# A copy in place of one of three transfers of V's block sums, halved query loads, and another written order in an attention and two-MLP kernel

## The chip, the cores and the metric

The kernel runs on one core of one Trainium2 chip. The metric is device time in microseconds (us) of one execution. Three runs of the kernel before gave 610.78, 613.39 and 611.55 us: the median is 611.55 us.

## The reference

Everything is float32. Attention with a narrow window and block summaries comes first, then two MLPs (scaling factors of the inputs left out):

```python
def _attn_ref(q, k, v):                      # (2, 8, 768, 64)
    k_sum = k.reshape(B, H, nb, 32, D).max(axis=3)      # 24 block maxima of K
    v_sum = v.reshape(B, H, nb, 32, D).mean(axis=3)     # 24 block means of V
    scores_l = scale * q @ k.T, kept where |i - j| < 16, else -1e9
    scores_s = scale * q @ k_sum.T + log(32)
    a = softmax(concat([scores_l, scores_s], -1))
    return a @ concat([v, v_sum], 2)

def _moe_ref(x, w_in, w_out):                # x (1536, 512), w_in (512, 2048)
    h = x @ w_in
    return (h * sigmoid(h)) @ w_out

def _moe2_ref(x, w_a, w_b, w_out):           # w_a, w_b (512, 1536)
    return (x @ w_a * (x @ w_b)) @ w_out
```

The heads of the attention's output are laid side by side to make the x of the first MLP, whose output is the x of the second.

## The kernel before

**Attention steps.** The attention is cut into 24 steps: 2 batches times 12 blocks of 64 queries, all 8 heads in a step. A step n is a string of small pieces, each a word in the table ORDER: `sc:n` (TensorE, "PE": scores, line 415, with the mask of some steps added by a product, line 409), `sm:n` (VectorE, "DVE": mask and row maximum), `ex:n` (ScalarE, "ACT": exponentials, line 459), `rs:n` (DVE: one over the row sum), `no:n` (GpSimd, "POOL", or DVE: scaling, line 474), `tr:n` (PE: transposes into `pt`, line 480), `pc:n` (copy of them into `pts`), `av:n` (PE: product with the values, line 495), `xh:n` and `xl:n` (the result split into a high and a low part). Scores of two steps share banks, and so do the products `av` of two steps.

**What must be there first.** K and Q arrive as 256 sequence rows at a time (`LKq`, `LQq`, `LQ`), are put in place by copies (`br`), transposed on PE (`tk`, `tq`, line 276, four transposes a word) and copied out in windows (`wk`) or scaled (`bq`, tile `qb`, or `qbm` for the second set). The block means of V come from four loads `LG:b:g` (line 329, two heads each, tiles `vg`), which `sv` sums partly on DVE or POOL (line 338: three halving additions, or one when four terms are left to PE), and which `mv` reduces on PE (line 352, tile `vsum`). `kv` then copies the 24 rows of means into the tile `vw0`.

**The value tiles.** Step n multiplies with `vw[n % 4]`: rows 0 to 95 are the window of V, loaded anew for each step (`LV`, line 369); rows 96 to 119 are the 24 block means of the batch. `kv` fills these in `vw0` alone; `PV:b:i` spreads them to `vw1`, `vw2`, `vw3` by a transfer inside the chip's memory on SyncE's queue ("SP", line 361). The tiles and their last rows live for the whole batch.

**The first MLP** is woven into the attention: `m1:i` (line 591, 12 matmuls of 512 columns; the first two units in halves of 256, `m1:1:0` and `m1:1:1`), `sg`, `gh`, `gl` (its activation, split in high and low), and `m2:i` (line 624, 12 matmuls). Their weights come as words that must be decoded: `LI`/`LO` load, `da` (ACT, line 535), `du` and `dj` (DVE) make a float, `hi` and `lo` split it; `SP` writes a decoded output weight back for the later blocks of tokens. `m1:i` needs the x parts of all eight steps of its block, a half only those of four.

**The order** of all this is the table ORDER near the top of the file, word by word; every engine and SP's queue takes its own instructions in that order, and nothing is moved later. `dm:i:y` puts four transposes of a constant into an unread bank on PE (`keep_warm`, line 926); `dm:i:n` does nothing. After the table's last word (`att`) comes the rest: the first MLP's last units, and the second MLP, in loops that the change does not touch.

Of the kernel before, what the change touches and what calls it, by code (L numbers as in the profile page):

```python
# [32 lines left out]
ex:1 sm:2 rs:1 ex:2 dm:2:n sc:0:n sc:3:s sm:3 mv:0:0:512:4 LG:0:2 LG:0:3 sv:0:3:4:v LQ:0:1 tq:0:1:0 ex:3 bq:0:1:0:v sm:0 ex:0
mv:0:1:0:1 mv:0:3:0:4 sv:0:2:1:p mv:0:2:0:1 kv:0:0:v tq:0:1:1 no:1:p bq:0:1:1:a tr:1 pc:1:a rs:3 pk:0:1:p sc:4:n LV:1 rs:2
rs:0 LI:1 no:3:p tr:3 sc:7:n sc:5:s sm:4 pc:3:v LV:3 dm:7:y LI:2 sm:7 du:in:1 da:in:1 no:2:p tr:2 PV:0:1 ex:4 PV:0:3 no:0:p
rs:4 no:4:p sm:5 av:3:n av:1:s tr:0 ex:7 LQ:0:2 rs:7 ex:5 pc:2:a xh:1:v xh:3:v xl:3 sc:6:n tq:0:2:0 LV:0 xl:1 tq:0:2:1 sm:6
pc:0:a dm:8:n du:in:2 dj:in:1 no:7:p tr:7 da:in:2 ex:6 LV:2 av:0:n bq:0:2:1:a tr:4 dj:in:2 PV:0:2 av:2:n pk:0:2:p bq:0:2:0:v
sc:11:n sc:9:s rs:5 dm:6:n no:5:p xh:0:a xl:0 rs:6 pc:7:a xh:2:a xl:2 sc:8:n LI:0 dm:11:n pc:4:a sc:10:s tr:5 sm:11 sm:9
no:6:p tr:6 hi:in:1:p sm:10 LV:7 av:7:n dm:9:n LV:4 av:4:s LV:5 lo:in:1:p ex:11 LV:6 pc:5:a av:5:n rs:11 no:11:p sm:8 xh:7:v
xl:7 pc:6:a da:in:0 xh:5:a av:6:n dm:4:n xh:6:a xh:4:a tr:11 LK:1:1 ex:8 su:10:v ex:10 m1:1:0 xl:4 ex:9 LI:4 xl:6 xl:5 m1:1:1  # L40
hi:in:2:v LQ:1:0 rs:10 du:in:0 dj:in:0 hi:in:0:v lo:in:0:v lo:in:2:p m1:2 ok:1 du:in:4 tk:1:1:1 sg:1:p gh:1:v gl:1:v tq:1:0:0
sg:2:p tk:1:1:0 tq:1:0:1 da:in:4 dj:in:4 hi:in:4:v LI:3 du:in:3 lo:in:4:v LI:7 LK:1:0 da:in:3 dj:in:3 bq:1:0:1:a rs:8
mk:1:1:0 du:in:7 m1:0:0 m1:0:1 no:8:p da:in:7 LK:1:2 LO:1 bq:1:0:0:a sg:0:v mk:1:1:1 pc:11:a wk:1:1:0:a no:10:p wk:1:1:1:a
dj:in:7 hi:in:7:v lo:in:7:p gh:2:p gh:0:v m1:4 gl:0:v tk:1:0:0 mk:1:0:0 tr:8 hi:in:3:a tk:1:2:0 rs:9 wk:1:2:0:a wk:1:0:0:a
pc:8:a tk:1:0:1 mk:1:0:1 gl:2:p no:9:v da:out:1 LI:13 sg:4:p da:in:13 LV:8 LI:6 lo:in:3:p LV:9 tk:1:2:1 mk:1:2:1 wk:1:2:1:a
# [1151 lines left out]
```

## Time and profile before

| what | value |
|---|---|
| median of three runs | 611.55 us |
| the profiled execution's own time | 610.3 us |
| its span, first to last instruction | 608.5 us |
| PE busy | 598.3 us (98%) |
| DVE busy | 390.2 us (64%) |
| ACT busy | 283.3 us (47%) |
| POOL busy | 270.9 us (45%) |
| bytes moved by DMA | 97.82 MB, mean 161 GB/s |
| granted clock of PE | 1.0 |

A busy share is a mean over stages that differ. PE's small share of idle time is what is left to win or to lose; where in the span it lies is read from the rows below.

### The profile page before, as it was taken

Reading aid. Unit: us, or ns where it says so; the run is one execution under the profiler, and the core shown is the slowest. Engines: PE = TensorE matmul, PEld = TensorE weight load, DVE = VectorE, ACT = ScalarE, POOL = GpSimd, SP = SyncE. Lnnn points to the kernel's source line nnn. Section 1 sums busy time; section 2 is a strip of 40 time slices with the busy share of each in tenths; the row PEclk is TensorE's granted clock in tenths of the full one; section 3 lists DMA queues with packets and bytes.
Section 4 is the critical chain, followed back from the end, with each engine's and each line's share of the span. In section 5 each row is a group of like instructions: output and inputs, shape, how many; then the busy total and the mean of one; then the engine's idle time right before and its main releaser. Section 6 shows DMA issues by size and latency. Waiting matters only on the chain.

```text
span 608.5 us, 10110 instructions
## 1 busy us (share of the span) xinstructions
PE 598.3 (98%) x3652; PEld 525.3 (86%) x3652; DVE 390.2 (64%) x775; ACT 283.3 (47%) x625; POOL 270.9 (45%) x265
## 2 busy tenths in 40 slices
PE   6999999999999999999999999999999999999997
PEld 6788888888788888888888999999999999988886
DVE  6889999878344444577576856694858567454212
ACT  5988778464445144545555313252423223234221
POOL 6745312123342222354457666392956657334220
PEclk9999999999999999999999999999999999999999
DMA  9999987883122427665664105362543512277303
GB/s 238 209 256 254 294 259 210 248 270 103 50 62 59 138 70 225 214 201 191 206 193 155 43 23 179 126 219 101 174 159 112 182 36 87 90 236 296 122 0 139
DMA packets 90538, 97.82 MB, mean 161 GB/s; under 512 B 39016, under 2 KB 68456, under 8 KB 90488
## 3 DMA queue, kind: packets, MB, share of 16 engines
q1 hardware_dynamic: 90344, 97.04, 52.7%
...
q10 hardware_dynamic: 144, 0.13, 0.1%
HBM read 73.79 MB, written 23.07 MB: 159 GB/s over the span
## 4 chain that ended last, share of the span: by engine, by line
PE 95%; DMA 2%; DVE 1%; SPq 1%; ACT 1%; issue 0%; DVEq 0%
PE h L591 22%; PE y L624 22%; PE bankh L835 14%; PE bankg L835 14%; PE ol L882 11%; PE o L858 5%; PE av L495 2%; PE pt L480 1%; PE sc L415 1%; DMA vg<-in_v_dram 1%; DMA st_in<-in_moe_w_in_dram 1%; DVE sm L445 1%; PE qt L276 1%; SPq L253 1%; ACT sm L459 0%; PE kt L276 0%
## 5 line engine op out<-in xcount | busy, mean ns | idle before, releaser
L591 PE MATMUL h<-x,w_in 128*128 128x512 f32 (+1 forms) x600 | 139.4, 383 | 0.0
L624 PE MATMUL y<-g,w_out 128*128 128x512 f32 x576 | 138.5, 391 | 0.0
L591 PEld LDWEIGHTS h<-x,w_in 128*128 128x128 f32 x600 | 108.3, 188 | 21.7 <-issue 0.3
L624 PEld LDWEIGHTS y<-g,w_out 128*128 128x128 f32 x576 | 107.4, 188 | 22.3 <-issue 0.2
L568 POOL TENSOR_TENSOR w_out<-re_out,w_out 128x512 fp32r<-128x512 f32 x38 | 53.9, 1419 | 109.9 <-ACT w_out L151 91.2
L882 PE MATMUL ol<-w_out,plh 128*128 128x512 f32 x188 | 57.8, 389 | 0.0
L606 DVE TENSOR_TENSOR g<-h,g 128x512 fp32r<-128x512 f32 x31 | 21.4, 690 | 42.3 <-ACT g L151 42.0
L568 POOL TENSOR_TENSOR w_out<-w_out,w_out 128x512 fp32r<-128x512 f32 x18 | 25.9, 1451 | 41.1 <-ACT w_out L151 29.9
L599 ACT ACTIVATE h<-h 128x512 f32<-128x512 f32 x31 | 18.1, 583 | 55.2 <-PE h L591 55.2
L800 POOL TENSOR_TENSOR ab<-sum,ab 128x384 f32<-128x384 f32 x24 | 27.3, 1146 | 33.4 <-DVE sum L797 33.4
L882 PEld LDWEIGHTS ol<-w_out,plh 128*128 128x128 f32 x188 | 35.3, 188 | 7.3
L151 ACT CAST w_out<-re_out 128x512 fp32r<-128x512 f32 x35 | 21.8, 621 | 32.9 <-issue 27.0
L871 DVE TENSOR_TENSOR pll<-pl,plh 128x1024 fp32r<-128x1024 f32 x12 | 17.4, 1449 | 30.5 <-ACT plh L870 30.5
L882 PE MATMUL ol<-w_out,pll 128*128 128x512 f32 x94 | 36.6, 389 | 0.0
L858 PE MATMUL o<-w_out,p 128*128 128x512 f32 x108 | 28.5, 393 | 0.0
L835 PE MATMUL bankh<-yhT,wab 128*128 128x384 f32 x96 | 28.2, 334 | 0.0
L545 DVE SCALAR_TENSOR_TENSOR w_out<-w_out,u_out 128x512 uint32<-128x512 uint32 x28 | 23.8, 855 | 5.3 <-ACT w_out L535 3.8
L778 ACT COPY sum<-bankh 128x384 f32<-128x384 f32 x12 | 5.8, 480 | 39.3 <-PE bankh L835 39.3
L474 POOL TENSOR_TENSOR sm<-sm,st 128x480 f32<-128x480 f32 x15 | 15.2, 1027 | 18.2 <-DVE st L470 12.5
L568 POOL TENSOR_TENSOR w_in<-w_in,w_in 128x512 fp32r<-128x512 f32 x10 | 13.4, 1341 | 22.1 <-DVE w_in L153 10.5
L818 ACT CAST p<-ab 128x384 fp32r<-128x384 f32 x12 | 6.2, 514 | 35.0 <-POOL ab L800 17.8
L858 PEld LDWEIGHTS o<-w_out,p 128*128 128x128 f32 x108 | 19.9, 187 | 2.8
...
## 6 DMA issues: line engine op xcount, KB each, us to landing
...
```

The lines of the kernel that those rows point to most:

```text
L151: nc.scalar.copy(o, i)
L545: nc.vector.scalar_tensor_tensor(bits, bits, 3, u_t.pop((kind, f)), op0=ALU.logical_shift_left, op1=ALU.bitwise_or)
L568: engine.tensor_tensor(w[:, 1], w32_t[kind, f], w[:, 0].bitcast(F32), op=ALU.subtract)
L591: nc.tensor.matmul(h_ps[i][:, cols], win_t[f][:, a, c * P:(c + 1) * P], x_t[n][:, steps, m, c, :], start=(idx == 0), stop=(idx == 3 * NK - 1))
L599: nc.scalar.activation(sg_t[i], ps, AF.Silu)
L606: engines[engine].tensor_tensor(g_t[i][:, 1], sg_t.pop(i), g_t[i][:, 0].bitcast(F32), op=ALU.subtract)
L624: nc.tensor.matmul(y_ps[n, c], wout_t[i][:, a, c * P:(c + 1) * P], g_t[i][:, m, :], start=(f == 0 and (a, m) == (0, 0)), stop=(f == N1 - 1 ...
L800: engines["v" if k == 6 else "p"].tensor_tensor(at, x, at, op=ALU.mult)
L835: nc.tensor.matmul((A, B)[b], weights(u, a, s, s + 1)[:, 0, c * P:(c + 1) * P], yc_t[q, y][m][:, c, :], start=(idx == 0 and not more), sto ...
L858: nc.tensor.matmul(o_ps[t], g[:, a, c:c + P], w[:, m], start=(begins and (a, m) == (0, 0)), stop=(ends and (a, m) == PARTS[-1]))
L871: nc.vector.tensor_tensor(l, x, h.bitcast(F32), op=ALU.subtract)
L882: nc.tensor.matmul(late_o[j], late_p[f][a][:, j * P:(j + 1) * P], wo2_t[N2 + f][:, m], start=(f == 0 and (a, m) == (0, 0)), stop=(f == N2 ...
```

## The change

It does four things. `put_vsum` may copy by an engine, and the word `pv:0:1:a` makes the copy into `vw1` of the first batch one of ACT; the transfers to `vw2` and `vw3`, and all three of the second batch, stay. The first queries are loaded as two transfers of four heads each (`LQq:0:0:0 LQq:0:0:1`), as the first keys were already. The table ORDER is written anew from end to end: other places, and at many words another engine (the last letter). And seven `dm` words have a `y` instead of four, which makes 12 more transposes.

```diff
 ORDER = """
-LKq:0:0:0 LKq:0:0:1 qz br:k:0:0:0:v c1 dm:0:y br:k:0:0:1:a tk:0:0:0 tk:0:0:1 dm:5:n c3 ok:0 LKq:0:2 LKq:0:1 mk:0:0:0
...
+c1 ok:0 qz dm:5:y LKq:0:0:0 LKq:0:0:1 LKq:0:2 c3 br:k:0:2:0:v br:k:0:2:1:v LKq:0:1 br:k:0:0:1:a dm:7:n br:k:0:0:0:a tk:0:0:1
...
-    def put_vsum(i):
-        nc.sync.dma_start(vw[i][KL:KK], vw[0][KL:KK])
+    def put_vsum(i, engine=None):
+        if engine:
+            copy(engine, vw[i][KL:KK], vw[0][KL:KK])
+        else:
+            nc.sync.dma_start(vw[i][KL:KK], vw[0][KL:KK])
...
-            "LQq": lambda b, t: load_raw("q", b, t, True), "LQ": lambda b, t: load_raw("q", b, t),
-            "LG": load_vg, "LV": load_vw, "PV": lambda b, i: put_vsum(i),
+            "LQq": lambda *a: load_quick("q", *a), "LQ": lambda b, t: load_raw("q", b, t),
+            "LG": load_vg, "LV": load_vw, "PV": lambda b, i: put_vsum(i), "pv": lambda b, *a: put_vsum(*a),
```

What this moves is shown at three places; the lines of the changed kernel are one to four higher than those of the kernel before.

**Place 1: SP's queue at the start**, from the first queries to the block sums. The digits in a name are kind, batch and piece (`vg01`: V, batch 0, heads 2 and 3; `raw_q02`: queries, batch 0, third piece). Before:

```order
L253 DMA st_q00_231<-in_q_dram 128x8x128
L329 DMA vg00_243<-in_v_dram 96x2x512
L329 DMA vg01_301<-in_v_dram 96x2x512
L329 DMA vg02_354<-in_v_dram 96x2x512
L329 DMA vg03_356<-in_v_dram 96x2x512
L256 DMA raw_q01_359<-in_q_dram 128x8x64 x2
...
L361 DMA vw1_99<-vw0_98 24x512
L361 DMA vw3_101<-vw0_98 24x512
L256 DMA raw_q02_518<-in_q_dram 128x8x64 x2
```

And with the change:

```order
L267 DMA st_q00_204<-in_q_dram 128x4x128 x2
L330 DMA vg01_249<-in_v_dram 96x2x512
L330 DMA vg02_268<-in_v_dram 96x2x512
L330 DMA vg00_321<-in_v_dram 96x2x512
L330 DMA vg03_365<-in_v_dram 96x2x512
L257 DMA raw_q01_376<-in_q_dram 128x8x64 x2
...
L365 DMA vw3_101<-vw0_98 24x512
L257 DMA raw_q02_543<-in_q_dram 128x8x64 x2
```

The first queries are two transfers, `vg00` goes from first to third of the four V loads, and `vw1` has no transfer any more; the third queries still stand behind a transfer of block sums.

**Place 2: the sums of V and step 1's scaling on POOL**, and what PE does with them. POOL before:

```order
L338 TENSOR_TENSOR vg01_301<-vg01_301 96x2x256
L338 TENSOR_TENSOR vg01_301<-vg01_301 96x2x128
L338 TENSOR_TENSOR vg01_301<-vg01_301 96x2x64
L338 TENSOR_TENSOR vg02_354<-vg02_354 96x2x256
L338 TENSOR_TENSOR vg02_354<-vg02_354 96x2x128
L338 TENSOR_TENSOR vg02_354<-vg02_354 96x2x64
L474 TENSOR_TENSOR sm1_306<-sm1_306,st0_102 128x480
```

POOL with the change:

```order
L339 TENSOR_TENSOR vg00_321<-vg00_321 96x2x256
L339 TENSOR_TENSOR vg03_365<-vg03_365 96x2x256
L339 TENSOR_TENSOR vg02_268<-vg02_268 96x2x256
L339 TENSOR_TENSOR vg02_268<-vg02_268 96x2x128
L339 TENSOR_TENSOR vg02_268<-vg02_268 96x2x64
L478 TENSOR_TENSOR sm1_312<-sm1_312,st0_102 128x480
```

POOL had the three additions of `vg01`, which go to DVE, and takes from DVE the single ones of `vg00` and `vg03`; step 1's scaling stands behind the sums in both. PE before:

```order
L352 MATMUL vsum00_349<-vg00_243,sel_93 120x128 x4
L276 MATMUL qt010_362<-ident_91,raw_q01_359 128x128 x4
L352 MATMUL vsum00_349<-vg01_301,sel_93 120x128
L352 MATMUL vsum00_349<-vg03_356,sel_93 120x128 x4
L352 MATMUL vsum00_349<-vg02_354,sel_93 120x128
L276 MATMUL qt011_389<-ident_91,raw_q01_359 128x128 x4
L480 MATMUL pt1_396<-ident_91,sm1_306 120x128 x4
```

PE with the change:

```order
L930 MATMUL idle_162<-ident_91 128x128 x4
L353 MATMUL vsum00_350<-vg00_321,sel_93 120x128 x4
L930 MATMUL idle_162<-ident_91 128x128 x4
L277 MATMUL qt010_379<-ident_91,raw_q01_376 128x128 x4
L353 MATMUL vsum00_350<-vg01_249,sel_93 120x128
L353 MATMUL vsum00_350<-vg03_365,sel_93 120x128 x4
L353 MATMUL vsum00_350<-vg02_268,sel_93 120x128
L277 MATMUL qt011_404<-ident_91,raw_q01_376 128x128 x4
L484 MATMUL pt1_415<-ident_91,sm1_312 120x128 x4
```

PE keeps its order there and gets two banks of idle transposes more; the means end with `vg02` in both.

**Place 3: ACT between the first queries' second set and the copies of the first transposes.** Before:

```order
L383 ACTIVATE qbm_144<-qt011_389 128x512
L151 COPY pts1_401<-pt1_396 120x512
L535 ACTIVATE w32_in1_469<-st_in1_424 128x512
L459 ACTIVATE sm4_450,st0_102<-sc4_407,st0_102 128x120 x2
L459 ACTIVATE sm4_450,st0_102<-sc4_408,st0_102 128x120 x2
L459 ACTIVATE sm7_462,st1_103<-sm7_462,st1_103 128x120 x4
```

With the change:

```order
L152 COPY vw0_98<-vsum00_350 24x512
L387 ACTIVATE qbm_161<-qt011_404 128x512
L152 COPY pts1_445<-pt1_415 120x512
L539 ACTIVATE w32_in1_450<-st_in1_411 128x512
L152 COPY vw1_99<-vw0_98 24x512
L463 ACTIVATE sm4_447,st0_102<-sc4_424,st0_102 128x120 x2
L463 ACTIVATE sm4_447,st0_102<-sc4_425,st0_102 128x120 x2
L152 COPY pts3_495<-pt3_440 120x512
L463 ACTIVATE sm7_497,st1_103<-sm7_497,st1_103 128x120 x4
```

ACT takes the copy of the means into `vw0` (DVE's before), the new copy into `vw1`, which stands behind the decoding of the first input weight, and the copy of step 3's transposes. On PE `av:1` now comes right behind `tr:3` and before the scores of steps 7 and 5; before, `av:3` and `av:1` stood together behind those scores.

## Rows read from the trace of the kernel before

**Rows 1.** Busy time by stretch: us and records of each engine, clock, DMA share, GB/s

```profile
0.00:40.00 40.00, 32.98 (x474) 27.96 (x475) 29.98 (x126) 30.42 (x116) 26.01 (x52) 1.00 0.99 225
40.00:550.00 510.00, 509.97 (x2931) 451.45 (x2930) 344.12 (x637) 237.68 (x490) 231.92 (x205) 1.00 0.52 159
...
60.00:100.00 40.00, 40.00 (x328) 33.38 (x327) 36.93 (x114) 31.56 (x80) 11.77 (x11) 1.00 0.94 269
```

**Rows 2.** Chain that ended last, in order of time: start us, us, what

```profile
23.77 2.63 ACT sm L459 x14
...
53.12 1.31 PE kt L276 x12
...
60.78 1.08 PE av L495 x32
61.87 1.80 PE sc L415 x64
```

**Rows 3.** Timeline, 11 to 22 us: start us, us, engine, line, operation, [idle before <-releaser]

```profile
11.43 1.17 POOL L153 COPY raw_q<-st_q 128x512 f32<-128x512 f32 x2 [0.94 <-DMA st_q<-in_q_dram]
14.40 1.05 PE L415 MATMUL sc<-kin,qb 64*64 64x120 f32 x32 [0.22 <-DVE qb L381]
14.48 5.68 POOL L338 TENSOR_TENSOR vg<-vg 96x512 f32<-96x512 f32 x6 [1.89 <-DMA vg<-in_v_dram]
20.13 0.98 POOL L474 TENSOR_TENSOR sm<-sm,st 128x480 f32<-128x480 f32 x1
21.16 0.65 PE L480 MATMUL pt<-ident,sm 128*120 128x128 f32 x4
```

**Rows 4.** POOL's groups by shape, 12 to 24 us: busy us, mean ns

```profile
L338 POOL TENSOR_TENSOR vg<-vg 96x512 f32<-96x512 f32 x2 | 2.5, 1266 | 1.9 <-DMA vg<-in_v_dram 1.9
L338 POOL TENSOR_TENSOR vg<-vg 96x256 f32<-96x256 f32 x2 | 2.0, 988 | 0.2
...
L338 POOL TENSOR_TENSOR vg<-vg 96x128 f32<-96x128 f32 x2 | 0.9, 451 | 0.2
```

**Rows 5.** Timeline of POOL and of DVE at 18.5 to 19 us

```profile
18.39 1.25 POOL L338 TENSOR_TENSOR vg<-vg 96x256 f32<-96x256 f32 x1
18.37 0.68 DVE L338 TENSOR_TENSOR vg<-vg 96x512 f32<-96x512 f32 x1
```

**Rows 6.** Timeline, 20 to 40 us: the block sums, the first products, the first MLP matmul

```profile
20.74 0.70 DVE L153 COPY vw<-vsum 24x512 f32<-24x512 f32 x1
21.46 1.68 SPq L361 DMA_DIRECT2D vw<-vw  x2
21.89 0.61 ACT L151 COPY pts<-pt 120x512 f32<-120x512 f32 x1
23.09 0.68 ACT L535 ACTIVATE w_in<-st_in 128x512 f32<-128x512 f32 x1 [0.58 <-DMA st_in<-in_moe_w_in_dram]
26.50 1.15 PE L495 MATMUL av<-pts,vw 120*64 120x64 f32 x32 [0.82 <-ACT sm L459]
27.99 0.47 PE L409 MATMUL sc<-mask_r,spread_r 66*128 66x240 f32 x2
28.39 0.64 PE L415 MATMUL sc<-kin,qbm 64*64 64x120 f32 x16
28.96 1.09 PE L276 MATMUL qt<-ident,raw_q 128*128 128x128 f32 x8
31.15 0.31 SPq L369 DMA_DIRECT2D vw<-in_v_dram  x1
35.38 1.15 PE L495 MATMUL av<-pts,vw 120*64 120x64 f32 x32
39.00 5.87 PE L591 MATMUL h<-x,w_in 128*128 128x256 f32 x36
```

**Rows 7.** Timeline, 72 to 75 us: PE behind the second y group; DVE's low half of `w_out2`

```profile
72.98 2.88 PE L591 MATMUL h<-x,w_in 128*128 128x512 f32 x12
73.75 0.68 DVE L568 TENSOR_TENSOR w_out<-w_out,w_out 128x512 fp32r<-128x512 f32 x1
```

More of the change, by code (lines that the diff above doesn't have):

```diff
@@ L33 @@
[L33 to L45, printed above, removed]
@@ new lines @@
+LO:3 SP:1 su:13:p LG:1:1 sv:1:1:1:p xl:8 m2:1 du:out:2 du:in:5 dj:out:2 LO:5 da:in:5 dj:in:5 hi:out:2:a gh:3:a du:out:3
+LG:1:2 lo:out:2:v m2:2 gl:3:v LI:8 hi:in:5:a lo:in:5:v da:out:3 dj:out:3 gh:6:v sg:7:p xh:10:a SP:2 da:out:4 m1:5 hi:out:3:p
+xl:10 sg:5:v LQ:1:1 gl:6:v lo:out:3:v LG:1:0 gh:4:a du:out:4 du:in:8 sv:1:2:1:v da:in:8 dj:out:4 hi:out:4:a lo:out:4:p
+dj:in:8 hi:in:8:a LO:6 m2:3 SP:3 gh:5:v gl:5:v ex:12 m1:13 lo:in:8:v m1:8 gl:4:v sv:1:0:1:v da:out:5 LG:1:3 tq:1:1:1 ex:14
+tq:1:1:0 du:out:5 LI:9 bq:1:1:1:a dj:out:5 bq:1:1:0:a du:out:6 hi:out:5:v rs:12 lo:out:5:v sv:1:3:1:v m2:4 sg:13:p rs:14
@@ new lines @@
+no:14:p LI:10 mv:1:0:256:1 du:in:10 SP:5 da:out:6 da:in:9 mv:1:2:256:1 dj:out:6 mv:1:3:0:1 kv:1:2:a sg:8:v gh:8:a LO:7 SP:4
+mv:1:1:0:1 kv:1:0:a hi:out:6:v LV:14 lo:out:6:v ex:15 du:in:9 dj:in:9 hi:in:9:v ex:13 lo:in:9:v m2:5 gl:8:v da:in:10 m2:6
+da:out:7 dj:in:10 gh:7:v tr:14 no:12:p pc:14:v hi:in:10:a lo:in:10:v tr:12 m1:9 pc:12:a LV:13 LO:9 SP:6 pk:1:1:a sc:18:n
+du:out:7 dj:out:7 hi:out:7:a sg:9:v sc:16:s LI:12 da:in:12 gh:9:a du:out:9 rs:15 sm:16 PV:1:2 rs:13 LV:12 sm:18 m1:10
+du:in:12 no:13:v LI:14 lo:out:7:p no:15:p dj:in:12 tr:15 av:12:n gl:7:p LO:8 gl:9:v da:out:9 dj:out:9 hi:in:12:a pc:15:v
@@ new lines @@
+PV:1:3 av:14:s m2:7 SP:7 xh:14:a lo:in:12:p xl:14 m1:12 du:out:8 LI:11 da:out:8 dj:out:8 hi:out:8:v xh:12:v lo:out:8:v xl:12
+du:in:11 da:in:11 dj:in:11 LV:15 tr:13 sg:12:v LO:11 sg:10:v gh:12:a gl:12:v m2:8 PV:1:1 pc:13:v av:15:n av:13:s hi:in:11:p
+lo:in:11:p da:out:11 SP:9 xh:15:a gh:10:v du:out:11 SP:8 dj:out:11 xl:15 LO:10 xh:13:a xl:13 hi:out:9:v da:out:10 lo:out:9:v
+LQ:1:2 SP:11 m1:11 gl:10:v sg:11:v du:out:10 sc:17:n sc:19:s dj:out:10 hi:out:10:a lo:out:10:v LO:15 sm:17 su:17:v SP:10 m2:9
@@ new lines @@
+hi:in:15:v lo:in:15:v SP:14 sg:14:p tr:16 lo:out:14:v m1:15 gh:14:a gl:14:v m2:14 du:out:15 dj:out:15 SP:15 pc:16:v
+hi:out:15:p lo:out:15:p first xh:17:v xh:18:v xl:18 xl:17 pk:1:2:a sg:15:v gh:15:v gl:15:v m1:18 sg:18:p sc:22:n sc:21:s
+sm:21 m2:15 RO:18 hR:18:v m1:19 yh:0:2 yh:0:3 RO:16 LV:21 RO:17 yh:0:1 sm:22 rs:19 LV:22 no:19:p tr:19 yh:0:0 hR:16:v lR:16:v
+m1:21 pc:19:a su:22:p ex:22 gh:18:v gl:18:v sc:20:n sc:23:s RO:19 rs:22 hR:17:v lR:17:v RO:20 no:22:p m2:16 m2:17 sg:21:p
+gh:21:p sm:20 ex:20 gl:21:p hR:19:v su:21:p sg:19:p ex:21 m1:24 sm:23 ex:23 lR:19:p rs:21 tr:22 no:21:v av:19:n LV:23 gh:19:p
@@ L79 @@
+hR:27:v gl:26:v lR:27:v att
 """
```

66 lines of the change are left out of this document (30 added, 36 removed).

## The prediction

> **What bounds the kernel now.** I read the busy time by stretch first. PE is busy for 32.98 of the first 40 us and for 509.97 of the 510 us behind them, at the full granted clock [rows 1]. So nothing is to be had behind 40 us except by taking PE work away, and a wait that the new order makes there costs its full length. In front of 40 us PE is idle for 40 - 32.98 = 7.0 us. Some of that is PE's first wait for its constant and for the first keys, whose transfers stand where they stood. Then I read the timeline of the first 40 us for what ended the other waits. The first queries' transpose waits for POOL's copy, which waited for the transfer and ran from 11.43 to 12.60; the scores start at 14.40 [rows 3]. PE's longest late wait is 0.82 us before the first value products at 26.50. The row blames ACT, but these products need the copied transposes (0.61 us from 21.89) and the block sums in `vw3` and `vw1`, whose two transfers SP issues from 21.46 to 23.14 [rows 6]: the last thing to come is a transfer, some 4.1 us after the second issue began (at about 22.3, the middle of the 1.68 us). This wait is what the copy by ACT is aimed at.
>
> The kernel's time is that of the span plus 1.8 us (610.3 against 608.5). The profiled execution is 1.25 us below the median of 611.55; I make the sum against the span and add its result to the median. A difference of 0.5%, 3.06 us, is about what a measurement of this kernel can tell from no change.
>
> **The change part by part.** Prices, all from rows: a transpose 1.31 / 12 = 0.109 us, so four take 0.44; the 16 records of a step's products 0.54, of its scores 0.45 [rows 2]; the masks 0.40 before scores (27.99 to 28.39) [rows 6]; an exponential with its read-out 2.63 / 7 = 0.38, so a step of four 1.50 [rows 2].
>
> *Idle transposes.* 12 x 0.109 = 1.3 us more PE work, all of it in front of 40 us. Eight stand between the sums of V and the first transposes of step 1, where PE will wait anyway (below), and one bank before the third queries' transposes, where it waits too; I cost them at nothing. Without that cover they cost 1.3.
>
> *Keys' copies.* The first keys are both copied by ACT and the third piece by DVE. ACT's 0.6 us more comes before a wait for a transfer that stays; nothing on the path.
>
> *Halved queries.* The second half lands when the whole did, so POOL's second copy begins at 11.43 instead of 12.0 and ends at 12.04; the transposes end at 12.7 (six more of them), ACT scales twice (0.61 each, as the copy of a bank [rows 6]) and the scores start at 14.1 instead of 14.40: 0.3 us gained, for now. If the halves were slower than the whole, it is 0.
>
> *Sums of V.* POOL began at 14.48, when the second load of V had come [rows 3]. Now it begins with `vg00`, which is third. When the third landed is bounded: behind 14.48, and not behind 17.1, when POOL, free at last, used it without waiting (14.48 + 2.60 for the three additions of `vg01`: 1.27 + 0.73 + 0.45 and gaps of 0.15; the 0.73 is twice the mean of 0.988 less 1.25 [rows 4, 5]). Two loads landed between the queries (11.43) and 14.48, some 1.5 us each, so I take 16.0 for the third and 17.5 for the fourth. Then `vg00` ends at 17.3, `vg03` at 17.5 + 1.27 = 18.8, and the three additions of `vg02` at 18.8 + 2.60 = 21.4. Step 1's scaling (0.98) ends at 22.4 and its transposes start at 22.45, where 21.16 stood [rows 3]. That is 1.3 us lost, and PE, with about 6 us of work between 14.1 and there, waits some 1.2 of it.
>
> POOL's second addition of `vg02` took 1.25 us where the same shape took 0.73; DVE ran an addition of its own over 18.37 to 19.05 [rows 5]. The Trainium skill, SBUF — State Buffer, states that DVE and GpSimd share one pair of ports as an exclusive lock, which a DVE operation with two SBUF inputs or in a two-port mode holds for its whole length; the trace agrees, with 0.52 us lost inside a DVE addition of 0.68. By that rule `no:0`, which the change gives to DVE in just that stretch, would stall POOL again, and the sum would be 0.5 us worse.
>
> *The copy by ACT.* The means end at 21.4 + 0.2; ACT copies them (0.70, DVE's price [rows 6]) until about 22.4, scales queries until 23.0, copies step 1's transposes until 23.6, decodes the first weight (0.68; its transfer had landed by 23.09 [rows 6]) until 24.3, and only then makes the copy into `vw1`. The trace has no such copy on ACT: 120x512 takes 0.61 there, 24x512 takes 0.70 on DVE [rows 6]; I take 0.65. `av:1` can start at 24.95. PE is through with steps 4 and 3 at 24.2, so it waits 0.75 us. Then `av:1`, the scores of 7 and 5 (0.90) and `tr:0` bring it to 26.85. `av:3` needs a transfer issued at 22.4, which lands at 22.4 + 4.2 = 26.6, and step 3's copy, now on ACT behind step 4's exponentials: 24.95 + 1.50 + 0.61 = 27.05. So `av:3` runs 27.05 to 27.6, not earlier than the 26.50 of before: the wait is not removed but cut into pieces.
>
> *The next transfer in line.* The third queries are needed at once after it (28.05, with an idle bank). Before, their transposes started at 28.96 [rows 6], behind other work; their transfer is issued right behind the block sums and no earlier than before. I take 28.9 and a wait of 0.85; if they had landed well before 28.96 it is 0.
>
> From there in PE's new order: `qt020` 0.44, step 6 with masks 0.85, `tr:4`, `qt021`, `tr:2` 1.31 to 31.5; `av:0` to 32.05; `tr:7` and `av:2` to 33.0; four steps' scores 1.80, `av:7`, `tr:5`, `tr:6` to 36.2. `av:4` needs `vw0` reloaded, which SP may issue once `av:0` is done: before, it was issued at 31.15 and used at 35.38 + 0.54, so 4.8 us later [rows 6]; now 32.05 + 4.8 = 36.85, a wait of 0.65. `av:4` and `av:5` end at 37.9. Here the new order is better: the first half of unit 1 starts now, 1.1 us before the 39.00 of before, and step 6's products are made under it. With half a unit at 5.87 / 4 = 1.47 (24 halves and 12 wholes in 36 records [rows 6]), `tr:11`, `av:6` and two key transposes (1.85) and the second half, unit 1 and these are done at 42.7. Before, the same work ended at 39.00 + 2.94 + 0.87 = 42.8.
>
> *Behind 40 us.* PE's work is the same. The tightest change I find is the third y group, which now follows the second at once, at 72.98 where unit 5 stood; its low weights end at 74.43 before [rows 7] and are needed at about 73.4. Only 1.0 us must be made up, four DVE instructions fewer stand ahead of them in the new order, and both the low halves of the first two groups are POOL's now, which is busy 11.77 of 40 us there [rows 1]. I cost it at 0; 1.0 is the other end.
>
> **Sum:** -0.1 us, so **611.4 us**. Best end: the four waits that I put in (1.2, 0.75, 0.85, 0.65) all vanish, -3.45 more. Worst end without a rival: `vg00` at 17.1 (+1.1), the addition at 1.25 (+0.5), 0.85 of it swallowed by the wait for the third queries, and +1.0 behind 40 us: +1.75.
>
> **Rivals.** *Faster:* the transfers land earlier than I bound them, and the new order's four waits shrink to nothing: 608.0 us. For it: the order has places for idle banks just there, and no row dates the third queries' landing. Against: three of the four hang on DMA, which is at 0.99 of its time in the first 40 us [rows 1], and the change takes only one small transfer off it. Chance 0.09.
>
> *Slower:* DVE becomes the bound from 60 to 100 us. It is busy 36.93 of 40 us there [rows 1], so a late start isn't made good, and every y group's weights pass it. If groups 2 to 5 each wait as long as the third would with its old time, 1.0 us, the four cost 4.0: 615.4 us. It decides from three such waits on. For it: the whole order is new there, and DVE has 3.1 us in reserve over 40. Against: the moves to POOL named above. Chance 0.16.
>
> *The change doesn't do what it says:* the copy into `vw1` replaces a transfer that nobody waits for alone, since `vw3` still comes by one. That is nearly my forecast; time 611.4, and its chance is in the middle case.
>
> **How the numbers follow.** No change: 0.75; faster by over 0.5%: 0.09; slower by over 0.5%: 0.16. The likeliest case reaches from -3.06 to +1.75 by its terms; to leave out no more than 2 in 10 the range takes in most of the slower rival, whose four waits end at 615.4, and most of the best end: 608.3 to 614.9 us.
>
> **What would show it.** In the new profile: scores at 14.1; the first `pt` at 22.4, after a POOL chain that begins at 16.0 and waits again for the fourth load; products in two rows, the first at about 25.0, before scores, and the next at 27.0; `h` at 37.9 instead of 39.00; PE idle 6 to 7 us in front of 40 us and nothing behind. If POOL begins its sums at 14.5, or the third queries are transposed before 28, the early part is better than I say. If PE is idle or its rows stretch between 60 and 110 us, the slower rival is at work. A span below 605.5 or above 611.6 would make the forecast of no change wrong.

## The result and the profile after

The changed kernel takes 616.46 us (median of 6 runs, 615.31 to 618.45), the kernel before 612.44 us beside it (6 runs, 610.78 to 613.53): ratio 1.0073, 95% interval [1.0053, 1.0093]. The forecast was 611.4 us with a range of 608.3 to 614.9. So the change costs about 4 us where I had forecast none. The profiled execution after has a span of 615.1 us against 608.5 before, 6.6 us more.

Busy time by stretch of the kernel after (columns as in [rows 1]):

```profile
0.00:40.00 40.00, 31.86 (x402) 26.76 (x402) 26.43 (x92) 26.57 (x100) 23.32 (x49) 0.96 0.85 196
40.00:550.00 510.00, 509.43 (x2996) 450.58 (x2987) 346.67 (x670) 238.58 (x496) 234.43 (x214) 1.00 0.53 157
20.00:27.00 7.00, 3.63 (x32) 3.21 (x31) 4.35 (x22) 6.38 (x34) 3.80 (x6) 1.00 0.70 180
27.00:31.00 4.00, 4.00 (x46) 3.05 (x49) 3.02 (x9) 3.85 (x13) 0.97 (x2) 0.57 0.56 125
60.00:80.00 20.00, 19.49 (x199) 16.21 (x199) 17.18 (x61) 12.11 (x27) 9.55 (x12) 1.00 1.01 267
```

Against [rows 1], PE is busy 31.86 instead of 32.98 us in front of 40 us, 1.1 less, in 402 records instead of 474, and the granted clock is 0.96 there; the DMA share falls from 0.99 to 0.85, and transfers such as the one into `vw3` are issued later (26.90 below). Two rows stand out. From 20 to 27 us PE works 3.63 of 7 us. From 27 to 31 it is busy throughout, but at a granted clock of 0.57, near the lower of its two levels (1.2 GHz). Behind 40 us it is idle for 0.57 us, 0.51 of them between 60 and 80.

PE in the timeline of the kernel after (start us, us, engine, line, operation, [idle before <-releaser]):

```profile
15.60 1.05 PE L419 MATMUL sc<-kin,qb 64*64 64x120 f32 x32 [0.22 <-ACT qb L387]
...
22.84 0.48 PE L353 MATMUL vsum<-vg,sel 96*120 96x128 f32 x2 [0.32 <-POOL vg L339]
...
26.81 0.66 PE L484 MATMUL pt<-ident,sm 128*120 128x128 f32 x4 [3.05 <-POOL sm L478]
27.22 0.63 PE L413 MATMUL sc<-mask_r,spread_r 66*128 66x240 f32 x2
27.78 1.08 PE L419 MATMUL sc<-kout,qbm 64*64 64x120 f32 x16
28.79 1.11 PE L484 MATMUL pt<-ident,sm 128*120 128x128 f32 x4
29.83 1.11 PE L499 MATMUL av<-pts,vw 120*64 120x64 f32 x16
...
32.43 0.69 PE L499 MATMUL av<-pts,vw 120*64 120x64 f32 x16
...
33.54 0.60 PE L277 MATMUL qt<-ident,raw_q 128*128 128x128 f32 x4
...
43.04 1.69 PE L595 MATMUL h<-x,w_in 128*128 128x256 f32 x12
...
46.55 3.80 PE L595 MATMUL h<-x,w_in 128*128 128x256 f32 x21
...
73.82 1.52 PE L628 MATMUL y<-g,w_out 128*128 128x512 f32 x6
```

The first `y` row in the kernel before:

```profile
67.54 5.60 PE L624 MATMUL y<-g,w_out 128*128 128x512 f32 x24
```

Step 1's transposes start at 26.81, where 21.16 stood [rows 3] and 22.45 was predicted, behind one wait of 3.05 us for POOL's scaling. Behind it the rows are stretched: 16 records of scores take 1.08 us and four transposes 1.11, the same forms farther down 0.64 and 0.65. The first products start at 29.83 (26.50 before, [rows 6]), `h` at 43.04 (39.00). The second half unit, behind the work that the new order puts between the halves (`tr:11`, `av:6`, two key transposes), starts at 46.55 and ends some 1.47 us later, at 48.0; the same work was done at 42.8 before. Of these 5.2 us, 1.2 are the later start of the first scores (15.60 against 14.40) and 4.0 are lost behind them. The first `y` row starts at 73.82 where 67.54 stood, 6.3 us later: 1.1 more are lost between unit 1 and it, 0.57 of them the idle time behind 40 us. From there to the end both take 541 us.

What POOL waited for is read from the other engines in the same timeline:

```profile
16.96 3.37 DVE L339 TENSOR_TENSOR vg<-vg 96x512 f32<-96x512 f32 x3
17.33 5.46 POOL L339 TENSOR_TENSOR vg<-vg 96x512 f32<-96x512 f32 x5 [3.05 <-DMA vg<-in_v_dram]
20.25 0.27 DVE L449 CUSTOM_DVE_ANT_0 sm<-sc,mask 128x120 f32<-128x120 f32 x1
...
20.56 0.40 ACT L463 ACTIVATE sm<-sm,st 128x120 f32<-128x120 f32 x1 [4.64 <-DVE st L449]
...
21.06 1.34 DVE L443 TENSOR_REDUCE st<-sc 128x2 f32<-128x240 f32 x4
24.25 0.41 DVE L443 TENSOR_REDUCE st<-sc 128x2 f32<-128x240 f32 x1 [1.85 <-ACT sm L463]
24.93 0.41 DVE L443 TENSOR_REDUCE st<-sc 128x2 f32<-128x240 f32 x1 [0.27 <-ACT sm L463]
25.26 0.15 DVE L473 TENSOR_REDUCE st<-st 128x4 f32<-128x8 f32 x1
25.77 2.04 POOL L478 TENSOR_TENSOR sm<-sm,st 128x480 f32<-128x480 f32 x2 [2.98 <-DVE st L473]
26.30 0.58 ACT L152 COPY vw<-vsum 24x512 f32<-24x512 f32 x1
26.90 0.88 SPq L365 DMA_DIRECT2D vw<-vw  x1
27.50 0.59 ACT L152 COPY pts<-pt 120x512 f32<-120x512 f32 x1
27.84 1.10 SPq L257 DMA_DIRECT2D raw_q<-in_q_dram  x2
28.68 0.61 ACT L152 COPY vw<-vw 24x512 f32<-24x512 f32 x1
```

POOL had ended its sums of V at 22.79 (17.33 + 5.46) and stood idle for 2.98 us. It lacked step 1's reciprocals, whose row sums DVE began at 25.26, behind the minima of step 3; and those waited for ACT's exponentials of step 0. ACT was late as well: it stood idle for 4.64 us, until DVE had the first minima of step 1 at 20.25, because DVE first added up `vg01`, from 16.96 on. From 20.56 ACT has no pause of note, and the means (26.30), step 1's transposes (27.50) and the copy into `vw1` (28.68) stand behind its sixteen exponentials. The transfer into `vw3` is issued right behind the means, at 26.90, and the third queries at 27.84. So there are two candidates: the place of one word (`rs:1`), or DVE's additions, which make ACT late.

### The profile page after: what moved, and what is told of

Its sections match the earlier page's. It is cut to its first block, busy times and chain, and to the rows that moved or that the text cites. A ratio compares the mean times of both kernels' runs of the same rounds, so it can differ in the third digit from the quotient of the medians.

```text
span 615.1 us, 10152 instructions
## 1 busy us (share of the span) xinstructions
PE 603.2 (98%) x3664; PEld 528.7 (86%) x3664; DVE 391.3 (64%) x776; ACT 283.5 (46%) x620; POOL 273.5 (44%) x272
## 4 chain that ended last, share of the span: by engine, by line
PE 93%; DMA 3%; ACT 1%; SPq 1%; DVE 1%; issue 0%; POOL 0%; DVEq 0%; ACTq 0%
PE y L628 21%; PE h L595 21%; PE bankh L839 14%; PE bankg L839 14%; PE ol L886 10%; PE o L862 5%; PE av L499 2%; PE pt L484 2%; DMA st_in<-in_moe_w_in_dram 2%; PE sc L419 1%; DMA st_q<-in_q_dram 1%; ACT sm L463 1%; SPq L267 1%; PE qt L277 1%; DVE vg L339 0%
## 5 line engine op out<-in xcount | busy, mean ns | idle before, releaser
L595 PEld LDWEIGHTS h<-x,w_in 128*128 128x128 f32 x600 | 108.5, 188 | 21.6 <-issue 0.4
L610 DVE TENSOR_TENSOR g<-h,g 128x512 fp32r<-128x512 f32 x31 | 21.4, 690 | 36.4 <-ACT g L152 36.1
L463 ACT ACTIVATE sm<-sm,st 128x120 f32<-128x120 f32 x52 | 19.9, 385 | 6.5 <-DVE st L449 6.4
```

Of the source, the lines that this page charges most:

```text
L463: nc.scalar.activation(sm[:, pr, :], x, AF.Exp, scale=-1.0, bias=st[:, 0, pr:pr + 1], accum_out=st[:, 1, pr:pr + 1])
L595: nc.tensor.matmul(h_ps[i][:, cols], win_t[f][:, a, c * P:(c + 1) * P], x_t[n][:, steps, m, c, :], start=(idx == 0), stop=(idx == 3 * NK - 1))
L610: engines[engine].tensor_tensor(g_t[i][:, 1], sg_t.pop(i), g_t[i][:, 0].bitcast(F32), op=ALU.subtract)
```

## The experiments

Each of the profiled executions starts a little differently: the first scores, which wait for the first keys and queries, started anywhere from 14.2 to 16.3 us, in either order (14.40 and 15.90 with the order of before). Behind the first `y` row all fourteen take 540.9 to 541.2 us, so what sets them apart lies ahead of it. I compare distances from the first scores, and times by their ratio to the kernel before.

| Kernel | ratio, 95% interval | scores | first `pt` | first products | `h` | `h` behind scores |
|---|---|---|---|---|---|---|
| before | 1 | 14.40 | 21.16 | 26.50 | 39.00 | 24.60 |
| after | 1.0073 [1.0053, 1.0093] | 15.60 | 26.81 | 29.83 | 43.04 | 27.44 |
| e1_rs | 1.0066 [1.0043, 1.0089] | 14.18 | 22.47 | 27.86 | 41.73 | 27.55 |
| e2_sv | 1.0032 [1.0016, 1.0048] | 15.17 | 24.61 | 27.33 | 40.16 | 24.99 |
| e3_rs_sv | 1.0040 [1.0015, 1.0064] | 14.84 | 24.26 | 27.18 | 40.00 | 25.16 |
| e4_whole | 1.0097 [1.0064, 1.0130] | 15.39 | 27.48 | 30.98 | 44.75 | 29.36 |
| e5_sums | 0.9989 [0.9973, 1.0006] | 14.46 | 21.89 | 25.08 | 37.75 | 23.29 |
| e6_transfer | 1.0106 [1.0084, 1.0129] | 14.76 | 23.99 | 26.95 | 42.02 | 27.26 |
| e7_before_copy | 0.9997 [0.9984, 1.0011] | 15.90 | 22.68 | 27.47 | 39.50 | 23.60 |
| e8_fill | 1.0066 [1.0045, 1.0087] | 16.25 | 27.47 | 30.02 | 42.82 | 26.57 |
| e9_sums_pc9 | 1.0008 [0.9992, 1.0023] | 14.82 | 22.25 | 25.20 | 37.90 | 23.08 |
| e10_pc9 | 1.0060 [1.0040, 1.0081] | 14.58 | 25.82 | 29.32 | 42.90 | 28.32 |
| e11_best_transfer | 1.0062 [1.0039, 1.0084] | 16.08 | 23.50 | 26.49 | 44.29 | 28.21 |
| e12_best | 1.0007 [0.9986, 1.0028] | 14.30 | 21.73 | 24.88 | 37.56 | 23.26 |

In the order of the change `h` begins with a half unit ahead of step 6's products, so its rows of `h` are not to be held against those of before (24.60, 23.60) without the work that it puts off. Counted to the end of unit 1, with the same work done (1.47 us behind the start of the second half; 42.8 for the kernel before), it is 28.4 us behind the scores before, 32.4 in the changed kernel, 30.0 in e2_sv, 30.2 in e3_rs_sv and 28.3 in e5_sums.

**One word alone: step 1's row sums ahead of step 3's minima.**

```
- ... sv:0:2:1:p sm:3 ex:3 rs:1 mv:0:1:0:1 ...
+ ... sv:0:2:1:p rs:1 sm:3 ex:3 mv:0:1:0:1 ...
```

> The changed kernel with one word moved: DVE computes step 1's row sums and reciprocals (rs:1) ahead of step 3's minima (sm:3), not behind them. In the changed kernel those minima wait until 24.25 us for ACT's exponentials of step 0, so rs:1 starts at 25.26, POOL's scaling of step 1 at 25.77 and PE's first pt row at 26.81, while POOL's sums of V end at 22.79. Theory A (that one word is the loss): rs:1 at 22.5, scaling 22.8 to 23.8, first pt at 23.85, 3.0 us earlier, and everything behind it too: the time falls by 2.5 to 3 us against the changed kernel, to within 0.3% of before (ratio 1.002 to 1.004). Theory B (ACT is the bound there: its exponentials start at 20.56 only, because DVE adds up vg01 from 16.96 to 20.33 ahead of step 1's minima, and ACT then has no pause until 30.8): the first pt row moves to 23.85, but the copies of the means (26.30) and of pt1 (27.50) stand behind ACT's exponentials, so the first products move from 29.83 by 0.5 us at most, and the time by less than 1 us (ratio 1.006 or more).

The time did not leave that of the changed kernel (1.0066 against 1.0073). The timeline of e1_rs:

```profile
19.16 0.40 ACT L463 ACTIVATE sm<-sm,st 128x120 f32<-128x120 f32 x1 [4.65 <-DVE st L449]
22.47 0.65 PE L484 MATMUL pt<-ident,sm 128*120 128x128 f32 x4
24.25 0.38 PE L413 MATMUL sc<-mask_r,spread_r 66*128 66x240 f32 x1 [1.12 <-DVE st L474]
...
26.19 0.64 PE L419 MATMUL sc<-kout,qbm 64*64 64x120 f32 x16 [0.88 <-DVE st L474]
...
27.86 1.12 PE L499 MATMUL av<-pts,vw 120*64 120x64 f32 x16
```

The first `pt` comes 8.3 us behind the scores instead of 11.2, as both theories said. PE then waits 1.12, 0.31 and 0.88 us at the next scores, and the products come 13.7 us behind the scores instead of 14.2. ACT starts its exponentials 5.0 us behind the scores, exactly as in the changed kernel (20.56 - 15.60). Theory A falls: the wait with the largest number hid another one behind it.

**DVE's additions behind the minima.**

```
- ... sc:1:s sv:0:1:1:v sm:1 ex:1 ... sm:2 ex:2 sm:0 LG:0:3 ...
+ ... sc:1:s sm:1 ex:1 ... sm:2 ex:2 sm:0 sv:0:1:1:v LG:0:3 ...
```

> The changed kernel with one word moved: DVE's three additions of vg01 stand behind the minima of steps 1, 2 and 0, not ahead of them; rs:1 stays behind step 3's minima. Theory B: step 1's minima start at 17.1 instead of 20.25, ACT's exponentials at 17.4 instead of 20.56, and steps 1, 2 and 0 are through on ACT at 21.9 without a pause; DVE adds until about 22.8 beside POOL, step 3's minima end at 23.5, its exponentials at 25.0; rs:1 at 23.7, scaling 24.0 to 25.0, first pt at 25.0 (1.8 earlier), the copy into vw1 ends at 27.5 and the first products start then, 2.3 us earlier than 29.83; time 2 to 3 us below the changed kernel, ratio 1.002 to 1.004. Theory A alone (only rs:1's place counts): first pt earlier by as much as step 3's exponentials are, and the products with it; it gives the same sign, so this run tells only whether ACT's late start counts; if it does not, products stay at 29.5 or later.

This takes back 0.41% (2.5 us); the first products come 12.2 us behind the scores instead of 14.2, as theory B said.

**Both words.**

> Both words moved: rs:1 right behind step 0's minima, then DVE's additions of vg01. First pt right behind POOL's sums of V and the scaling: POOL free at 22.8, pt at 23.85. By theory B the products are bound by ACT (exponentials of four steps until 24.9, then the means, the queries, pt1, the decode and the copy into vw1) and start at 27.0 to 27.5 as in the run with the additions alone moved: time within 0.7 us of that run. By theory A the two moves add up: 3 us more than that run. Together they should take back 2.5 to 4 of the 4 us: ratio 1.000 to 1.003.

With both, the time is that of the additions alone (the intervals overlap almost wholly) and the products come 12.3 us behind the scores: `rs:1` adds nothing once ACT is on time. In its timeline:

```profile
16.52 0.40 ACT L463 ACTIVATE sm<-sm,st 128x120 f32<-128x120 f32 x1 [1.35 <-DVE st L449]
...
22.41 1.57 PE L353 MATMUL vsum<-vg,sel 96*120 96x128 f32 x12 [1.74 <-DVE vg L339]
...
27.18 0.69 PE L499 MATMUL av<-pts,vw 120*64 120x64 f32 x16 [0.45 <-ACT vw L152]
```

ACT starts 1.7 us behind the scores, not 5.0. But DVE's additions now hold the means until 22.41, and 0.4% is still missing. The runs of e3_rs_sv differ by their mean granted clock: four at 0.999 or 1.0, the profiled one among them, took 612.29 to 612.84 us, about as the kernel before beside them (median 612.17), and six at 0.997 or 0.994 took 614.86 to 618.15. So the missing 0.4% is in executions whose clock fell, of which no trace is kept. A mean of 0.997 is worth at most 0.003 x 611 = 1.8 us (an estimate from the runs' own numbers), and even those at 0.997 took 2.3 us more or above, so the clock alone doesn't explain it. In e2_sv seven runs of ten were at 0.999 or 1.0, with a median of 614.25; of the changed kernel's six none was.

**The first queries by one transfer.** `LQq:0:0:0 LQq:0:0:1` becomes `LQq:0:0`.

> The changed kernel with the first queries loaded by one transfer again (POOL still copies them in two halves). In the changed kernel the second half landed 1.3 us later than the whole did before (POOL's second copy at 12.74 against 11.43 for the first copy before), the scores start at 15.6 instead of 14.4, and the third load of V is there at 17.33. Theory C (the second issue delays this and every later transfer): POOL's copies at 11.4 and 12.0, scores at 14.3, the third load of V at 16.0, first pt 1.3 earlier (25.5), time 1.0 to 1.5 us below the changed kernel (ratio about 1.005). Rival: the bytes are the same, the later loads land when they did, DVE's additions and minima hold the rest: scores earlier, first pt and the time unchanged (within 0.4 us).

Theory C falls: the scores start at 15.39, and the time is no better (1.0097, its interval overlaps that of the change). The halved load is not the loss; the 1.2 us by which the scores were late in the profile after are the scatter of the start. This run shows something else, in the view of one tile (instructions of `vg`: duration min/median/max in ns), first e4_whole:

```profile
L339 DVE TENSOR_TENSOR vg<-vg x3: 1241/1380/1542, 16.8 to 19.7; 96x512 f32<-96x512 f32 x1, 96x256 f32<-96x256 f32 x1, 96x128 f32<-96x128 f32 x1
```

and the kernel after:

```profile
L339 POOL TENSOR_TENSOR vg<-vg x5: 450/1318/1432, 17.3 to 22.3; 96x512 f32<-96x512 f32 x3, 96x256 f32<-96x256 f32 x1, 96x128 f32<-96x128 f32 x1
L339 DVE TENSOR_TENSOR vg<-vg x3: 676/1245/1380, 17.0 to 19.1; 96x512 f32<-96x512 f32 x1, 96x256 f32<-96x256 f32 x1, 96x128 f32<-96x128 f32 x1
```

and the kernel before:

```profile
L338 DVE TENSOR_TENSOR vg<-vg x2: 679/682/686, 12.9 to 18.4; 96x512 f32<-96x512 f32 x2
```

DVE's largest addition takes 0.68 to 0.69 us both with POOL not adding (at 12.9 in the kernel before) and where it begins ahead of POOL's (at 18.37 there [rows 5], at 16.96 in the changed kernel); then it is POOL's that is stretched. Where a POOL addition is already running, the ones with half and a quarter of its elements take 1.25 to 1.38 us, about one of POOL's (1.27 alone, [rows 4]), and in e4_whole the three take 4.2 us together.

**The sums of V by the engines of before**, with `rs:1` ahead of step 3's minima and the rest of the change kept.

```
- sc:1:s sv:0:1:1:v sm:1 ... sv:0:0:4:p mv:0:0:512:4 sm:2 ex:2 sm:0 ... sv:0:3:4:p ... ex:3 rs:1 mv
+ sc:1:s sv:0:1:1:p sm:1 ... sm:2 ex:2 sv:0:0:4:v mv:0:0:512:4 sm:0 rs:1 ... sv:0:3:4:v ... ex:3 mv
```

> The changed kernel with the sums of V by the engines of before: POOL adds up vg01 and then vg02 (three additions each), DVE vg00 and vg03 (one each, behind the minima of steps 2 and 0), and rs:1 behind step 0's minima. The changed kernel's loads, halved queries, copy by ACT and the rest of its order stay. Theory B (the loss is DVE's and ACT's late start, made by who adds up V, and POOL's five additions behind the third load): POOL adds from about 14.4 to 20.2, scales step 1 until 21.2, first pt at 21.3 (26.81 in the changed kernel, 24.26 with both words moved); ACT's fourth step of exponentials ends at 22.5 instead of 24.1, the copy into vw1 at 25.5 instead of 27.1: first products at 25.5, h at about 38.5, time 1.5 to 2 us below the run with both words moved, 0.999 to 1.002 of before. Rival: the rest of the new order is what costs, and the time stays at 1.003 or more.

The whole loss is gone: 0.9989, against 1.0073, some 5.1 us. Its timeline:

```profile
13.56 5.51 POOL L337 TENSOR_TENSOR vg<-vg 96x512 f32<-96x512 f32 x6
19.17 1.30 POOL L476 TENSOR_TENSOR sm<-sm,st 128x480 f32<-128x480 f32 x1
...
25.08 0.69 PE L497 MATMUL av<-pts,vw 120*64 120x64 f32 x16 [0.71 <-ACT vw L150]
...
27.26 0.69 PE L497 MATMUL av<-pts,vw 120*64 120x64 f32 x16
...
37.75 1.69 PE L593 MATMUL h<-x,w_in 128*128 128x256 f32 x12
...
41.27 4.98 PE L593 MATMUL h<-x,w_in 128*128 128x256 f32 x28
...
63.32 0.67 ACT L537 ACTIVATE w_in<-st_in 128x512 f32<-128x512 f32 x1 [0.80 <-DMA st_in<-in_moe_w_in_dram]
63.90 0.57 ACT L150 COPY pts<-pt 120x512 f32<-120x512 f32 x1
...
64.52 0.53 PE L417 MATMUL sc<-kin,qb 64*64 64x120 f32 x11 [1.47 <-ACT pts L150]
```

POOL begins at 13.56, with the first load of V, and not with the third. Products at 25.08 and 27.26 and `h` at 37.75 are close to the prediction's 24.95, 27.05 and 37.9. That `h` starts 1.25 us earlier than before is no gain: with the work put between the halves, unit 1 ends at 42.7 (41.27 + 1.47), where the kernel before had 42.8. Farther on PE waits 1.47 us at 64.52 for a bank that ACT copies out (step 9's transposes), behind a decode of `w_in13` that waits for its transfer.

**The copy back to a transfer**, in the kernel with both words: `pv:0:1:a` becomes `PV:0:1`.

> The run with both words moved (rs:1 and the additions of vg01), and the copy into vw1 made by a transfer again, issued where ACT's copy stood in the order. Theory: with av:1 put ahead, the copy is needed: ACT keeps the means until 24.8, the transfer into vw1 is issued at 24.8 to 25.7 and lands some 4.1 us behind its issue, at 29; the first products start at 29 instead of 27.2, those of step 3, whose transfer is now second, at 30.3 instead of 29.4, the third queries are 0.9 later; time 1 to 2 us above that run. Rival (my own from the prediction): the copy stands for a transfer that nobody waits for alone; products of step 3 and the time stay within 0.5 us.

It costs 0.66% (some 4 us by the ratios, 2.8 by the medians; its one run at a mean clock of 1.0 took 615.89 us, against 612.29 to 612.84 in e3_rs_sv). I had expected the first products to be late, and they were not: they start at 26.95, the transfer being there 2.4 us behind its issue at 24.55. The price stands farther back in SP's queue:

```profile
26.01 0.77 SPq L363 DMA_DIRECT2D vw<-vw  x1
...
30.67 0.69 PE L497 MATMUL av<-pts,vw 120*64 120x64 f32 x16 [1.48 <-DVE st L447]
...
32.60 0.63 PE L275 MATMUL qt<-ident,raw_q 128*128 128x128 f32 x4 [0.66 <-DMA raw_q<-in_q_dram]
```

The transfer into `vw3` is now the second, behind an input weight's load as well, and issued 1.2 us later, PE waits 1.48 us in front of step 3's products, and 0.66 us for the third queries, which are behind both. The releaser named is DVE, but the missing input is the transfer: the last landing on the DMA semaphore that PE waits for there comes at 30.42, and PE's wait for it ends at 30.45.

**The copy alone, in the kernel before**, made by POOL behind step 0's scaling.

```
- ... tr:2 PV:0:1 ex:4 PV:0:3 no:0:p ...
+ ... tr:2 ex:4 PV:0:3 no:0:p pv:0:1:p ...
```

> The kernel before with one thing of the change alone: the block sums reach vw1 by a copy instead of a transfer, by POOL behind the scaling of step 0, where POOL is idle from 24.86 to 26.51. The transfer into vw3 is then the first in SP's queue (issued at 21.46 instead of 22.4), and the third queries' two are 0.9 earlier. Theory (the 0.82 us wait at 26.50 is for the transfer into vw3, the second of two): step 3's products start at 25.6 instead of 26.5, the copy is ready by 25.6 for step 1's, and the time falls by 0.5 to 0.9 us: ratio 0.9985 to 0.999. Rival: the time of before is set there by the third queries or by ACT's copies, and the gain is given back by 40 us: ratio 1.000.

The products come 11.6 us behind the scores instead of 12.1 and `h` 1.0 earlier, but the time is 0.9997 with an interval that takes in both theories. In the two profiled executions nothing of it reaches the end: from the first scores the span takes 594.1 us in both. Whether it does in the mean stays open.

**The wait filled with idle transposes**: `dm:20:y` to `dm:25:y` ahead of `tr:1` in the changed kernel.

> The changed kernel with six more banks of idle transposes (24, 2.6 us of PE work) ahead of step 1's transposes, in the stretch where PE waited 3.05 us. Behind that wait the rows of the changed kernel are stretched to half speed from 27.2 to 30.5 (granted clock 0.87 and 0.96 in the windows 20 to 30 and 30 to 40). Theory D (the wait lowers the clock, and this costs time of its own): no stretched rows, clock 1.00 in both windows, first pt as before, first products at 29.3 (ACT's copy) instead of 29.83, h 1.0 to 1.3 us earlier, time 0.7 to 1.3 us below the changed kernel (ratio 1.0055). Rival: at full clock PE only waits longer for ACT's copies, and the time stays within 0.4 us.

The stretch from 27 to 31 us in e8_fill, against the granted clock of 0.57 above:

```profile
27.00:31.00 4.00, 3.06 (x57) 2.43 (x60) 3.79 (x11) 3.92 (x11) 1.51 (x3) 1.00 0.36 81
```

The clock stays at its full level, the products come 0.46 us and `h` 0.87 us earlier behind the scores. So the lowered clock cost about 0.9 us of this stretch, by one execution of each kernel. In that of e8_fill the clock fell elsewhere: 0.52 from 10.5 to 14.0 us, ahead of the scores. The time (1.0066 against 1.0073) is too coarse to confirm it. Most of PE's lost speed lay in front of a wait for ACT's copy (0.51 us at 30.02) anyway.

**ACT's copy of step 9's transposes ahead of its decodes**, with the sums repaired and in the changed kernel alone:

```
- ... du:in:13 da:out:0 dj:out:0 da:in:13 ... dj:in:13 pc:9:a ...
+ ... du:in:13 pc:9:a da:out:0 dj:out:0 da:in:13 ... dj:in:13 ...
```

> The run with the sums of V by the engines of before, and one more word moved: ACT's copy of step 9's transposes (pc:9) stands ahead of its decodes of w_out0 and w_in13, not behind them. In the run without that move h starts at 37.75, 1.25 us earlier than before the change, but PE then waits 1.47 and 0.23 us at 63 to 66: the scores of steps 14 and 12 need the bank that holds step 9's transposes, and ACT's copy out of it (63.90) stands behind the decode of w_in13, which waits for its transfer until 63.32. Theory E (that copy is what gives the early gain back): the copy is made at 61.9 to 62.5, no wait at 63, and the time falls by 1.4 to 1.8 us: ratio 0.9960 to 0.9970 of before. Rival: the weights' transfers bound that stretch anyway, PE waits for them a few us later, and the ratio stays at 0.999.

> The changed kernel with only that word moved (pc:9 ahead of ACT's decodes of w_out0 and w_in13). Its waits at 68 to 70 are 0.28 and 0.23 us (stalls of 0.54 and 0.44 against the usual distance of rows). Theory E: both go, and the time falls by 0.5 to 0.9 us against the changed kernel: ratio 1.006 (1.0073 without). The rest of the loss, in front of 30 us, stays. Rival: no change (ratio 1.007).

The first missed: 1.0008, where 0.9960 to 0.9970 was expected from an early gain that the end of unit 1 doesn't show. The second's 1.0060 is the number expected, but not for the reason given, and its interval takes in 1.0073. In both the waits moved to the next copy of the same queue; in e9_sums_pc9:

```profile
64.90 1.15 PE L497 MATMUL av<-pts,vw 120*64 120x64 f32 x32 [1.03 <-ACT pts L150]
```

(0.91 us in e10_pc9, more than the 0.51 of the two waits that it replaced), and neither time can be told from that without the move.

**The copy back to a transfer, with both repairs.**

> The run with both repairs (sums of V by the engines of before, pc:9 ahead), with the copy into vw1 made by a transfer again: what the change's first part is worth where nothing else is late. In the run with both words moved this cost 2.8 us: the first products were not later (the transfer landed 2.4 us behind its issue), but the second transfer, into vw3, and the third queries stood 1.2 us further back in SP's queue, and the products of step 3 came 1.3 us later, the third queries 2.1. Theory F (the copy pays by SP's queue, not by the products it feeds): step 3's products 1 to 1.5 us later than with the copy, the third queries 1 to 2 us later, time 1 to 2.5 us above the run with both repairs. Rival (from the prediction: the copy replaces a transfer that nobody waits for alone): within 0.5 us of it.

1.0062 against 1.0008: the copy is worth 0.54%, some 3.3 us, in the order of the change, where in the order of before nothing was to be measured. The profiled execution shows 1.45 us of waiting in front of step 3's products, 0.86 us for the third queries, and a lowered clock behind them (0.61 from 30 to 38 us).

**A version meant to beat both**: `pc:10:a` ahead too, and no idle bank in front of the third queries.

> A version meant to beat both: the run with both repairs, with ACT's copy of step 10's transposes (pc:10) also put ahead of the decodes of w_out0 and w_in13, and without the bank of idle transposes (dm:4, 0.44 us) ahead of the third queries. In the run with both repairs h starts at 37.90 and PE waits 1.03 us at 63.9 for the copy of step 10's transposes, at 64.25 behind a decode at 62.18, one at 62.88 and two casts. Theory E: no wait above 0.2 us behind 40, h at 37.5, and 1.0 to 1.4 us less than that run: ratio 0.997 to 0.999 of before. Rival: the weights' transfers hold that stretch, PE waits for w_out0 or w_in6 instead, ratio 1.000 to 1.002.

It doesn't: 1.0007. `h` starts at 37.56 and the copies' waits are gone, but then PE waits for a weight:

```profile
68.53 7.75 PE L626 MATMUL y<-g,w_out 128*128 128x512 f32 x33 [0.65 <-POOL w_out L570]
```

## Why the prediction was wrong

The step that failed is **Sums of V**, with the figure for ACT in **The copy by ACT** that rests on it. I followed POOL's queue load by load and left DVE's out, though the change gives DVE three additions. Three things were missed there.

- On DVE the additions of `vg01` stand ahead of step 1's minima. They delayed them from 1.1 us behind the scores (15.49 in the trace of before) to 4.7, and ACT's exponentials with them. I let ACT copy the means at 21.6, as soon as they were there; it was free at 26.3. The runs e1_rs, e2_sv and e3_rs_sv separate this from the place of `rs:1`, and moving the additions alone gives back 2.5 us of time.
- POOL starts with the third load, so all five additions are late. I took 16.0 for it, bounded by 17.1; it was 17.33 in the profile, 15.8 in e1_rs and 16.5 in e4_whole, so the value was fair and its bound a little short for the scatter of the start. The chain ended at 22.79 instead of 21.4. Together with DVE's share this is the rest: e5_sums, with the engines of before, takes back 0.5% more than e3_rs_sv. Against the four runs of e3_rs_sv at full clock it is only 0.6 us (medians 611.93 and 612.54, with 612.43 and 612.17 for the kernel before beside them), so most of that 0.5% is lost in runs where the clock fell as well; how the two hang together is not shown.
- The scaling needs step 1's reciprocals, and I had them ready. Their row sums were begun 2.5 us behind the end of POOL's sums (25.26 against 22.79), since DVE's minima of step 3 waited 1.85 us for ACT to be through with step 0, whose scores lie in the same two PSUM banks (`sc0`). The Trainium skill, PSUM — Partial Sum Buffer, PSUM bank collisions raise a hardware error, states that two engines must not access one bank at once on the same 32 partitions, two reads included. The trace agrees as far as it shows the wait: DVE's two minima start at 24.25 and 24.93, each behind ACT.

The rule that I had weighed there, the shared ports of DVE and GpSimd, was read for POOL alone. The Trainium skill, SBUF — State Buffer, SBUF: two separate sides, lets whichever starts first hold the ports for its whole instruction. The trace agrees: now DVE lost, from its second addition on (1.38 and 1.25 us), and in e4_whole, where POOL began first, from its first on (1.54). The place that I named for it, step 0's scaling on DVE, hardly mattered: it took 0.75 us at 27.57, and POOL's scaling beside it 0.99, as long as in the kernel before.

The other steps, one by one:

- *Halved queries*: not shown to gain or lose; "scores at 14.1" lies at the early edge of a scatter from 14.2 to 16.3. In the profiled executions e5_sums takes 2.2 us longer from the first scores to the end than the kernel before (596.3 against 594.1), and yet its time is the same; its scores may come earlier in the mean, which two starts with the order of before can't settle.
- *Behind the first `pt`*: near once that was on time. From 22.45 to `h` I had 15.45 us; e5_sums has 15.86, and its rows at 25.08, 27.26 and 37.75 are within 0.25 of the forecast. That it comes so close is partly luck: its first `pt` is 0.56 us earlier than mine, PE waits 0.44 and 0.71 us in front of the first products, and of the 0.85 and 0.65 that I had farther on there is nothing. The change has 16.23, with 0.9 of it from the clock. I had given the clock no term: in the trace of before PE's longest wait is 1.6 us and the clock is 1.00 throughout [rows 1].
- *The third queries' wait* (0.85) wasn't there (33.54, no wait), nor the 0.65 for `vw0` (41.96).
- *Idle transposes at nothing*: not tried by itself; in e5_sums PE runs through from 17.3 to the first `pt` with eight of them, so that cover was thin, but ACT bounds what follows. My wait of 1.2 us in front of the first `pt` doesn't follow from its own figures: from 14.1 to 22.45 it is 8.35 us, about 6 of them work. Only the best end uses it; 3.05 was measured.
- *Behind 40 us at 0, 1.0 as the other end*: 0.57 us idle, and not at the third y group but where ACT copies out step 9's transposes behind a decode. With the early part repaired it is 1.7 us in the profiled execution.

Of the rivals, *slower* had the sign and nearly the time (615.4), by the wrong mechanism: DVE is not the bound from 60 to 100 us, it is what stood in the wrong order at 17. *The copy replaces a transfer nobody waits for alone* is refuted in the order of the change: undoing it costs 2.8 to 4.0 us. *Faster* did not come even with the sums repaired: unit 1 ended at 42.7, as forecast, against 42.8 in the kernel before. What I said would show an error did show it: the first `pt` at 26.81 instead of 22.4.
